# Down projection on two 64-row array tiles, paired denominators, and an earlier release of K's weights

## The chip, the cores and the metric

The kernel runs on one core of one Trainium2 chip. The metric is the device time of one execution in microseconds (us). "Before" ran at 523.56 us (median of 3 runs, 523.36 to 523.85). A ratio is the mean time of one kernel's runs over that of the other's runs in the same rounds, so it is not quite the ratio of the medians quoted beside it.

Engines are named as in the profile: PE is TensorE (PEld its weight loads), DVE VectorE, ACT ScalarE, POOL GpSimd, SP SyncE.

## The reference, cut to what matters

A linear-attention block and a GeGLU feed-forward on the same normalised input, added to the input. S = 2048 tokens, D = 576, 32 heads of 18, F = 4608, all bfloat16.

```python
xn  = layernorm(x)
q, k, v = split(xn @ wqkv);  pq, pk = phi(q), phi(k)
kv  = einsum("bhsd,bhse->bhde", pk, v);  z = sum over s of pk
att = ((pq @ kv) / (pq @ z)) @ wo
ffn = (gelu(xn @ w_gate) * (xn @ w_up)) @ w_down
out = x + att + ffn
```

## The kernel before: what the change and the argument touch

First, all tokens are normalised, K and V are reduced to the small matrix of each head and Q is made. Then there are four stages of 512 tokens, each a gate/up stage (L313, 36 feature blocks) and a down stage. The down stage multiplies the gated features `hT` with `w_down`, 36 steps, and adds five steps of attention: queries `pqT`, divided by their denominators, times `m_sb`, the product of each head's small matrix with `wo`.

The gate/up stage uses TensorE as two tiles of 64 rows. A `_Unit` has two outputs in two banks of PSUM, the memory that TensorE writes its results to. In its first phase the low rows work on output 0 and the high rows on output 1; in its second phase they change places. A relay (an empty instruction on another engine) keeps one tile from writing a bank before the other has left it.

```python
        def p1(self):                              # first phase
            for kt in self.first:
                self.mm(0, LO, kt, ...)
                last = self.mm(1, HI, kt, ...)
            self.turn = self.relay.nop()           # waits for `last`
        def p2(self):                              # second phase waits for the relay
            for kt in self.then:
                m = self.mm(1, LO, kt, ...)
                self.mm(0, HI, kt, ...)
```

The down stage uses the whole array, and so do the single denominators and the M products that are slipped in:

```python
    def down_tile(sc, j, hooks):                   # [cut]
        for hf in range(2):
            for f in range(NF):                    # 36 matmuls, 128 rows, 288 columns
                if f in todo: todo[f](acc_bank)    # an M product or a denominator
                nc.tensor.matmul(acc, lhsT=hT[:, f, ...], rhs=wd_sb[:, f, hs], ...)
            for c in range(NCH):                   # 5 more: attention
                nc.tensor.matmul(acc, lhsT=pqT[:rows, c, ts_], rhs=m_sb[:rows, c, hs], ...)
```

At the very start, the first x tiles are loaded from SP's queue and K's weights from ACT's. K's weights wait for a two-element write into their destination, which stands behind a large zero-fill on VectorE:

```python
    load_x(0, 1); load_x(1, 1); load_x(2, 2)               # SP queue: 144, 144, 288 KB
    nc.vector.memset(wqkv_sb[HP:P, 4, :], 0.0)             # 0.78 us
    nc.vector.memset(wqkv_sb[0:1, 0, D:D + 2], 0.0)        # 0.06 us
    load_w(1, nc.scalar)                                   # K's weights, 576 + 72 KB
```

## Time and profile before

| | before |
|---|---|
| median, us | 523.56 |
| TensorE's share of the chain that ended last | 97% |
| four gate/up stages | 71.33 and three times 70.04 us |
| four down stages | 42.49, 41.42, 41.42, 40.40 us |
| first gate matmul, from the span's start | 71.59 us |

The stage times are worked out from the starts of single matmuls in the trace: from the first matmul of one stage to that of the next. The views in the prediction show how TensorE's stream makes up the kernel.

### The profile page before, as it was taken

To read this page: it belongs to the slowest core of one execution; us is meant where nothing else is said; L and a number is where in the kernel's file an instruction comes from. 1 tells how busy PE (TensorE), PEld (TensorE's weight loads), DVE (VectorE), ACT (ScalarE), POOL (GpSimd) and SP (SyncE) were. 2 spreads that over 40 slices of the span, in tenths; PEclk is the share of its full clock that TensorE was granted. 3 is DMA by queue.
4 is the path that set the end of the run, shared out by engine and by line. 5 is a ranking of instruction groups with operands and counts; after the bars stand their busy time and mean duration, and the time that the engine had idled before them with its cause. 6 is when DMAs were issued, how large, how long until landed. Compare 5 with 4: busy or idle time off the path is not lost.

```text
span 521.7 us, 10641 instructions
## 1 busy us (share of the span) xinstructions
PE 516.1 (99%) x4498; PEld 313.5 (60%) x4498; DVE 250.9 (48%) x436; ACT 143.1 (27%) x293; POOL 35.2 (7%) x55
## 2 busy tenths in 40 slices
PE   7999999999999999999999999999999999999997
PEld 6777755555587754444577744444777544445775
DVE  7996565876358323433388133333584233433101
ACT  6898442332320013323200032232000123322000
POOL 2021000211001100000012000000011000000000
PEclk9999999999999999999999999999999999999999
DMA  8334609899500045555300155555100355440000
GB/s 279 62 64 118 154 25 264 254 269 266 157 12 13 13 124 155 144 156 160 93 13 13 41 166 145 155 156 155 29 23 13 103 161 158 140 134 2 13 11 24
DMA packets 106282, 57.89 MB, mean 111 GB/s; under 512 B 13370, under 2 KB 105722, under 8 KB 106234
## 3 DMA queue, kind: packets, MB, share of 16 engines
q1 hardware_dynamic: 105626, 56.55, 38.8%
q8 instruction: 35, 0.57, 0.5%
q10 hardware_dynamic: 608, 0.66, 0.4%
q14 instruction: 13, 0.11, 0.1%
HBM read 52.86 MB, written 2.36 MB: 106 GB/s over the span
## 4 chain that ended last, share of the span: by engine, by line
PE 97%; DMA 1%; ACT 1%; DVE 0%; issue 0%
PE ps_all L313 55%; PE ps_all L677 27%; PE ps_all L289 4%; PE ps_all L682 4%; PE ps_all L245 3%; PE ps_all L342 3%; DMA wqkv_sb<-in_A_wqkv_dram 1%; PE ps_all L451 1%; PE ps_all L433 0%; PE ps_all L659 0%; ACT xnT L234 0%; ACT L114 0%; ACT phi_e L265 0%; ACT phi_e L269 0%; DVE hT L273 0%; DVE res L685 0%
## 5 line engine op out<-in xcount | busy, mean ns | idle before, releaser
L313 PE MATMUL ps_all<-xnT,wg 64*128 64x512 bf16 x1152 | 272.6, 376 | 0.0
L313 PE MATMUL ps_all<-xnT,wu 64*128 64x512 bf16 x1152 | 271.8, 376 | 0.0
L648 DVE TENSOR_TENSOR hT<-ps_all,gl 128x512 bf16<-128x512 f32 x144 | 99.5, 691 | 161.9 <-ACT gl L647 161.2
L647 ACT ACTIVATE gl<-ps_all 128x512 f32<-128x512 f32 x144 | 86.1, 598 | 314.3 <-PE ps_all L313 297.4
L313 PEld LDWEIGHTS <-wu 64*128 64x128 bf16 x1152 | 108.3, 94 | 66.3
L313 PEld LDWEIGHTS <-wg 64*128 64x128 bf16 x1152 | 108.3, 94 | 66.1
L677 PE MATMUL ps_all<-wd_sb,hT 128*128 128x288 bf16 x1152 | 147.0, 286 | 0.0
L677 PEld LDWEIGHTS <-hT 128*128 128x128 bf16 x1152 | 112.3, 98 | 30.6 <-issue 1.3
L475 DVE RECIPROCAL den_sb<-den_sb 126x128 f32<-126x128 f32 (+1 forms) x80 | 68.3, 911 | 0.5
L685 DVE TENSOR_TENSOR res<-ps_all,x_sb 128x288 bf16<-128x288 f32 x32 | 14.7, 458 | 88.0 <-PE ps_all L682 88.0
L313 PE MATMUL ps_all<-xnT,wr 64*128 64x512 bf16 x288 | 55.1, 376 | 0.0
L478 POOL TENSOR_TENSOR pqT<-pqT,den_sb 126x512 bf16<-126x512 bf16 (+3 forms) x25 | 24.2, 966 | 317.3 <-DVE den_sb L475 279.4
L682 PE MATMUL ps_all<-m_sb,pqT 126*128 126x288 bf16 (+1 forms) x160 | 24.9, 285 | 0.0
L313 PEld LDWEIGHTS <-wr 64*128 64x128 bf16 x288 | 14.4, 94 | 16.9 <-issue 0.7
L245 PE MATMUL ps_all<-wqkv_sb,xnT 128*128 128x288 bf16 x160 | 22.5, 286 | 0.9 <-DMA wqkv_sb<-in_A_wqkv_dram 0.8
L289 PE MATMUL ps_all<-hT,xn 128*128 128x288 bf16 (+4 forms) x176 | 22.4, 275 | 0.0
L289 PEld LDWEIGHTS <-xn 128*128 128x128 bf16 (+1 forms) x176 | 17.5, 102 | 4.1
L245 PEld LDWEIGHTS <-xnT 128*128 128x128 bf16 x160 | 15.4, 98 | 6.9 <-issue 1.4
L682 PEld LDWEIGHTS <-pqT 126*128 126x128 bf16 (+1 forms) x160 | 15.5, 97 | 4.1
L342 PE MATMUL ps_all<-xnT,wqkv_sb 128*126 128x512 bf16 (+1 forms) x70 | 17.4, 378 | 0.0
L273 DVE SCALAR_TENSOR_TENSOR hT<-ps_all,phi_e 128x288 bf16<-128x288 f32 x32 | 13.2, 450 | 4.6 <-ACT phi_e L269 4.0
L265 ACT ACTIVATE phi_e<-ps_all 128x288 f32<-128x288 f32 x32 | 12.9, 410 | 3.6 <-PE ps_all L245 2.1
(68 smaller groups left out, 173.8 us busy)
## 6 DMA issues: line engine op xcount, KB each, us to landing
wg<-in_B_w_gate_dram SPq DMA_DIRECT2D x72, 256.0 KB, 2.9
wu<-in_B_w_up_dram SPq DMA_DIRECT2D x72, 256.0 KB, 3.5
wd_sb<-in_B_w_down_dram SPq DMA_DIRECT2D x12, 432.0 KB, 4.6
wr<-in_B_w_gate_dram SPq DMA_DIRECT2D x72, 32.0 KB, 2.7
wr<-in_B_w_up_dram SPq DMA_DIRECT2D x72, 32.0 KB, 3.1
out_dram<-res SPq DMA_DIRECT2D x15, 144.0 KB, 1.8
x_sb<-in_A_x_dram SPq DMA_DIRECT2D x3, 576.0 KB, 7.1
wqkv_sb<-in_A_wqkv_dram SPq DMA_DIRECT2D x2, 576.0 KB, 4.7
```

What stands on the lines that cost most here:

```text
L245: nc.tensor.matmul(ps_all[:, k_bank(n, hf), :HALF], lhsT=xnT[:, kt, n * P:(n + 1) * P], rhs=wqkv_sb[:, kt, D + hf * HALF:D + (hf + 1) * HALF],
L273: nc.vector.scalar_tensor_tensor(out=out_, in0=ps, scalar=0.0, in1=e, op0=ALU.max, op1=ALU.add)
L289: nc.tensor.matmul(ps_all[:m, b, col:col + w], lhsT=xn[:, n, j0:j0 + m], rhs=pk[:, n, d0:d0 + w], start=(n == 0 and col == 0), stop=(n == ...
L313: return nc.tensor.matmul(self.outs[i], lhsT=self.lhs(i, rows, kt), rhs=self.rhs(i, rows, kt), start=start, stop=stop, skip_group_check=True,)
L342: nc.tensor.matmul(ps, lhsT=wqkv_sb[:, kt, q0:q0 + rows], rhs=xnT[:, kt, sc * SC:(sc + 1) * SC], start=(kt == 0), stop=(kt == KT - 1),)
L475: nc.vector.reciprocal(out=d[:, h:h + P], in_=d[:, h:h + P])
L478: nc.gpsimd.tensor_tensor(out=pqT[:rows, c, cols], in0=pqT[:rows, c, cols], in1=d, op=ALU.mult)
L647: nc.scalar.activation(out=gl[:], in_=ps_all[:, b[0], :], func=ACT.Gelu_apprx_tanh)
L648: nc.vector.tensor_tensor(out=hT[:, GUB * k + i, :], in0=ps_all[:, b[1], :], in1=gl[:], op=ALU.mult)
L677: nc.tensor.matmul(acc, lhsT=hT[:, f, j * P:(j + 1) * P], rhs=wd_sb[:, f, hs], start=(f == 0), stop=False,)
L682: nc.tensor.matmul(acc, lhsT=pqT[:rows, c, ts_], rhs=m_sb[:rows, c, hs], start=False, stop=(c == NCH - 1),)
L685: nc.vector.tensor_tensor(out=res[:, hs], in0=acc, in1=x_sb[:, n, hs], op=ALU.add)
```

## The change

The intent: keep TensorE in its two-tile mode through the down stages too, so that it need not change mode at each end; pair the denominators; and let K's weights leave earlier by putting the large zero-fill behind them. Cut to its core:

```diff
-    nc.vector.memset(wqkv_sb[HP:P, 4, :], 0.0)
     nc.vector.memset(wqkv_sb[0:1, 0, D:D + 2], 0.0)
     load_w(1, nc.scalar)
+    nc.vector.memset(wqkv_sb[HP:P, 4, :], 0.0)
[cut]
+    nc.vector.memset(pqT[HP:P, NCH - 1, 2 * SC:], 0.0)
+    for t in (kvT, m_sb, wo2):
+        nc.vector.memset(t[HP:P, NCH - 1, :], 0.0)
[cut: den_mm, m_stage and down_tile removed]
+    def down_unit(n, b):          # one token tile: 41 steps, two halves of 288 columns
+        [cut: lhs and rhs, the slices of hT, pqT, wd_sb and m_sb for one row tile]
+        steps = range(NF + NCH)
+        return _Unit([ps_all[:, b + i, :HALF] for i in range(2)], lhs, rhs, nc.scalar, steps, steps)
+    def down_last(n, b):          # the last token tile stays on the whole array [cut]
+    def down(sc):
+        p = [banks.tiles[(banks.i + 2 * k) % 8] for k in range(4)]     # bank pairs, oldest first
+        [cut: n0, last]
+        u = [down_unit(n0 + j, p[j % 3]) for j in range(TPC - last)]
+        [cut: hooks, one table per token tile]
+        if sc == 0:
+            ms = [m_unit(c, p[3 - c % 2]) for c in range(NCH)]
+            hooks[0] = run_turns(6, ms, 9, 3, m_copy)   # from step 9, every 6; 2nd phase 3 steps later
+        [cut: one pair of denominators per token tile, first phase at step 4, second 3 steps later]
+        u[0].p1(hooks[0])
+        for j in range(1, len(u)):
+            u[j].p1(hooks[j])
+            u[j - 1].p2()
+            down_out(n0 + j - 1, u[j - 1].outs)
+        u[-1].p2()
```

More of the change, by code (lines that the diff above doesn't have):

```diff
@@ L316, in mm, with p1 @@
             )
-        def p1(self):
+        def p1(self, hooks=()):
             for kt in self.first:
+                if kt in hooks:
+                    hooks[kt]()
                 self.mm(0, LO, kt, kt == self.first[0], False)
@@ L323, in p1, with p2 @@
             tc.add_manual_dep(self.turn.ins, last.ins.name, SYNC, reason="the row tiles take turns on a bank")
-        def p2(self):
+        def p2(self, hooks=()):
             for kt in self.then:
+                if kt in hooks:
+                    hooks[kt]()
                 m = self.mm(1, LO, kt, False, kt == self.then[-1])
@@ L446, in den_evac, with part, den_pair @@
         den_sb[sc, c] = d
-    def den_mm(sc, c, bank):
-        rows = DH * HCH[c]
-        ps = ps_all[:rows, bank, :]
-        nc.tensor.matmul(ps, lhsT=zrep[:rows, c, :rows], rhs=pqT[:rows, c, sc * SC:(sc + 1) * SC], start=True, stop=True)
-        den_evac(sc, c, ps)
-    def den_pair(items, outs):
+    def part(r, c):
+        return slice(r.start, P if c == NCH - 1 else CR) if r is HI else r
+    def den_pair(items, outs, relay):
         rows = DH * HCH[items[0][1]]
-        def part(r):
-            return slice(r.start, min(r.stop, P if rows <= P - HP + 8 else rows))
         return _Unit(
             outs,
-            lambda i, r, kt: zrep[part(r), items[i][1], :rows],
-            lambda i, r, kt: pqT[part(r), items[i][1], items[i][0] * SC:(items[i][0] + 1) * SC],
-            nc.sync, first=(0,), then=(0,),
+            lambda i, r, kt: zrep[part(r, items[i][1]), items[i][1], :rows],
+            lambda i, r, kt: pqT[part(r, items[i][1]), items[i][1], items[i][0] * SC:(items[i][0] + 1) * SC],
+            relay, first=(0,), then=(0,),
         )
@@ L532 @@
     todo += [(4.0, lambda n: nc.vector.memset(x_sb[0:1, n, 0:2], 0.0), 4)]
-    todo += [(4.01, lambda n: load_x(n, 4), n) for n in (4,)]
-    todo += [(4.02, lambda n: load_w(0), 0)] + [(4.03, lambda n: load_x(n, 4), n) for n in (8, 12)]
+    todo += [(4.01, lambda n: load_x(n, 4), 4), (4.02, lambda n: load_w(0), 0)]
+    todo += [(4.03, lambda n: load_x(n, 4), n) for n in (8, 12)]
     todo.sort(key=lambda x: x[0])
@@ L641, in gu_pair @@
             items = DEN_PAIRS[k - DEN_FROM]
-            den = den_pair(items, [ps_all[:DH * HCH[c], banks.next(), :] for _, c in items])
+            den = den_pair(items, [ps_all[:DH * HCH[c], banks.next(), :] for _, c in items], nc.sync)
             den.p1()
@@ L652, in gu_pair, with m_unit, m_copy @@
                 den_evac(dsc, c, ps)
-    def m_stage(c, acc_bank):
+    def m_unit(c, b):
+        rows = DH * HCH[c]
+        return _Unit(
+            [ps_all[:rows, b + i, :HALF] for i in range(2)],
+            lambda i, r, kt: kvT[part(r, c), c, :rows],
+            lambda i, r, kt: wo2[part(r, c), c, i * HALF:(i + 1) * HALF],
+            nc.scalar, first=(0,), then=(0,),
+        )
+    def m_copy(c, u):
         rows = DH * HCH[c]
         for hf in range(2):
-            b = (acc_bank + 2 + (2 * c + hf) % 6) % 8
-            hs = slice(hf * HALF, (hf + 1) * HALF)
-            nc.tensor.matmul(
-                ps_all[:rows, b, :HALF], lhsT=kvT[:rows, c, :rows], rhs=wo2[:rows, c, hs], start=True, stop=True,
-            )
-            nc.scalar.copy(out=m_sb[:rows, c, hs], in_=ps_all[:rows, b, :HALF])
@@ L664, in down_tile, with lhs, rhs @@
-    def down_tile(sc, j, hooks):
-        n = sc * TPC + j
+            nc.scalar.copy(out=m_sb[:rows, c, hf * HALF:(hf + 1) * HALF], in_=u.outs[hf])
+    def down_unit(n, b):
+        sc, j = divmod(n, TPC)
+        ts_ = slice(n * P, (n + 1) * P)
+        def lhs(i, r, kt):
+            return hT[r, kt, j * P:(j + 1) * P] if kt < NF else pqT[part(r, kt - NF), kt - NF, ts_]
+        def rhs(i, r, kt):
+            hs = slice(i * HALF, (i + 1) * HALF)
+            return wd_sb[r, kt, hs] if kt < NF else m_sb[part(r, kt - NF), kt - NF, hs]
+        steps = range(NF + NCH)
+        return _Unit([ps_all[:, b + i, :HALF] for i in range(2)], lhs, rhs, nc.scalar, steps, steps)
@@ L666, in down_tile, with down_out @@
+    def down_out(n, outs):
+        res = fwork.tile([P, D], BF16, name="res")
+        for hf in range(2):
+            hs = slice(hf * HALF, (hf + 1) * HALF)
+            nc.vector.tensor_tensor(out=res[:, hs], in0=outs[hf], in1=x_sb[:, n, hs], op=ALU.add)
+        nc.sync.dma_start(out_view[:, n, :], res[:])
+    def down_last(n, b):
         ts_ = slice(n * P, (n + 1) * P)
         res = fwork.tile([P, D], BF16, name="res")
-        last = n == NS - 1
         for hf in range(2):
             hs = slice(hf * HALF, (hf + 1) * HALF)
-            todo = hooks.pop(0) if hooks else {}
-            acc_bank = banks.next()
-            acc = ps_all[:, acc_bank, :HALF]
+            acc = ps_all[:, b + hf, :HALF]
@@ L674, in down_tile @@
             for f in range(NF):
-                if f in todo:
-                    todo[f](acc_bank)
                 nc.tensor.matmul(
-                    acc, lhsT=hT[:, f, j * P:(j + 1) * P], rhs=wd_sb[:, f, hs], start=(f == 0), stop=False,
-                )
+                    acc, lhsT=hT[:, f, (n % TPC) * P:(n % TPC + 1) * P], rhs=wd_sb[:, f, hs], start=(f == 0), stop=False)
             for c in range(NCH):
@@ L682, in down_tile @@
                 nc.tensor.matmul(
-                    acc, lhsT=pqT[:rows, c, ts_], rhs=m_sb[:rows, c, hs], start=False, stop=(c == NCH - 1),
-                )
+                    acc, lhsT=pqT[:rows, c, ts_], rhs=m_sb[:rows, c, hs], start=False, stop=(c == NCH - 1))
             nc.vector.tensor_tensor(out=res[:, hs], in0=acc, in1=x_sb[:, n, hs], op=ALU.add)
-            if last:
-                nc.sync.dma_start(out_view[:, n, hs], res[:, hs])
-        if not last:
-            nc.sync.dma_start(out_view[:, n, :], res[:])
+            nc.sync.dma_start(out_view[:, n, hs], res[:, hs])
@@ new lines, in den_norm_all, with run_turns, end, den_out @@
+    def den_norm_all(sc, c):
+        return lambda: den_norm(sc, c, 0, 1)()
+    def run_turns(step, units, first, gap, done):
+        hooks = {}
+        for i, u in enumerate(units):
+            hooks[first + step * i] = u.p1
+            def end(u=u, i=i):
+                u.p2()
+                done(i, u)
+            hooks[first + step * i + gap] = end
+        return hooks
+    def down(sc):
+        p = [banks.tiles[(banks.i + 2 * k) % 8] for k in range(4)]
+        n0 = sc * TPC
+        last = sc == NSC - 1
+        u = [down_unit(n0 + j, p[j % 3]) for j in range(TPC - last)]
+        hooks = [{} for _ in range(TPC)]
+        if sc == 0:
+            ms = [m_unit(c, p[3 - c % 2]) for c in range(NCH)]
+            hooks[0] = run_turns(6, ms, 9, 3, m_copy)
+        if not last:
+            items = [[(sc + 1, 0), (sc + 1, 1)], [(sc + 1, 2), (sc + 1, 3)]]
+            if (sc + 1, NCH - 1) in den_sb:
+                hooks[3][4] = den_norm_all(sc + 1, NCH - 1)
+            else:
+                items.append([(sc + 1, NCH - 1), (sc + 2, NCH - 1)])
+            for k, it in enumerate(items):
+                pair = den_pair(it, [ps_all[:DH * HCH[c], p[3] + i, :] for i, (_, c) in enumerate(it)], nc.scalar)
+                def den_out(_, unit, it=it):
+                    for (dsc, c), ps in zip(it, unit.outs):
+                        den_evac(dsc, c, ps)
+                    for dsc, c in it:
+                        if dsc == sc + 1:
+                            den_norm_all(dsc, c)()
+                hooks[k + 1] = run_turns(0, [pair], 4, 3, den_out)
+        u[0].p1(hooks[0])
[4 more added lines that the diff above has]
+        u[-1].p2()
+        down_out(n0 + len(u) - 1, u[-1].outs)
+        if last:
+            down_last(NS - 1, p[0])
+        banks.i += 2
@@ L699 @@
             load_wd_slice()
-        hooks = [{6 * c_: (lambda b, c_=c_: m_stage(c_, b)) for c_ in range(NCH)} if sc == 0 else {}]
-        if sc + 1 < NSC:
-            for c_ in range(NCH):
-                def dn(b, c=c_, nsc=sc + 1):
-                    if (nsc, c) not in den_sb:
-                        den_mm(nsc, c, (b + 2) % 8)
-                    den_norm(nsc, c, 0, 1)()
-                hooks.append({0: dn})
-        for j in range(TPC):
-            down_tile(sc, j, hooks)
+        down(sc)
 _INS = ['A_x', 'A_wqkv', 'A_wo', 'B_x', 'B_w_gate', 'B_w_up', 'B_w_down']
```

## The prediction

> **What bounds the kernel now.** I read three views: the page for shares, the chain of work that ended last for stages, and the timeline for single instructions. From the page, the chain's shares and the three largest rows (line, engine, operation, output from inputs, shapes, count, then busy us, mean ns of one, idle before):
>
> ```profile
> PE 97%; DMA 1%; ACT 1%; DVE 0%; issue 0%
> L313 PE MATMUL ps_all<-xnT,wg 64*128 64x512 bf16 x1152 | 272.6, 376 | 0.0
> L677 PE MATMUL ps_all<-wd_sb,hT 128*128 128x288 bf16 x1152 | 147.0, 286 | 0.0
> L677 PEld LDWEIGHTS <-hT 128*128 128x128 bf16 x1152 | 112.3, 98 | 30.6 <-issue 1.3
> ```
>
> TensorE's matmul stream is the end of the kernel: 97% of the chain, no idle time before the large groups. The gate and up projections (L313) already run on two 64-row tiles; the down projection (L677 and L682) uses the full array. So only two things can help: fewer or closer matmul slots, or an earlier start. The chain (start us, length us, what) around one down stage and its neighbours:
>
> ```profile
> 185.48 70.04 PE ps_all L313 x648
> 255.51 4.52 PE ps_all L677 x36
> 260.03 0.62 PE ps_all L682 x5
> 260.65 0.22 PE ps_all L451
> 260.86 4.41 PE ps_all L677 x36
> ```
>
> Here 36 down matmuls take 4.41 us, 122.5 ns each, and 648 gate and up matmuls take 70.04 us, 216.2 ns a pair. The first group after the gate stage takes 4.52, not 4.41: changing to the full array costs about 0.1. The timeline shows both sides of that change and what follows it on the other engines:
>
> ```profile
> 255.14 0.38 PE L313 MATMUL ps_all<-xnT,wg 64*128 64x512 bf16 x1
> 255.45 1.15 PE L677 MATMUL ps_all<-wd_sb,hT 128*128 128x288 bf16 x8
> 255.56 0.60 ACT L647 ACTIVATE gl<-ps_all 128x512 f32<-128x512 f32 x1 [0.27 <-PE ps_all L313]
> 256.19 0.69 DVE L648 TENSOR_TENSOR hT<-ps_all,gl 128x512 bf16<-128x512 f32 x1 [0.17 <-ACT gl L647]
> ```
>
> A pair would be followed 0.216 later; the down matmul comes 0.31 later, so about 0.095 is the change. The last gate/up unit's PSUM banks stay in use until 256.19 + 0.69 = 256.88, which matters below. At the start of the kernel the timeline has:
>
> ```profile
> 0.80 1.28 ACT L114 ACT_TABLE_LOAD   x1 [0.80 <-PEq L725]
> 1.05 0.78 DVE L119 MEMSET wqkv_sb<- 64x864 uint32 x1 [1.05 <-PEq L725]
> 1.86 0.06 DVE L120 MEMSET wqkv_sb<- 1x1 uint32 x1
> 1.95 0.44 ACTq L109 DMA_DIRECT2D wqkv_sb<-in_A_wqkv_dram  x1
> 6.65 0.24 DVE L234 COPY xnT<-ps_all 128x256 bf16<-128x256 bf16 x1
> 7.41 0.77 PE L245 MATMUL ps_all<-wqkv_sb,xnT 128*128 128x288 bf16 x5 [0.79 <-DMA wqkv_sb<-in_A_wqkv_dram]
> ```
>
> K's weights are issued at 1.95, just after the one-element write ended at 1.92 and while the table load was still running to 2.08; so the write, behind a 0.78 us memset, releases them and not the table load that the chain names. They land at 7.37 and the first K matmul starts at 7.41. From 12.0 us on, the chain is nothing but TensorE up to the last matmul.
>
> **What the Trainium skill says.** (1) "TensorEngine Tiling (Array Packing)", section Key Properties: changing the tiling mode drains TensorE. The trace agrees: about 0.095 us going in, and about as much coming out (the matmul after the last L682 one starts 0.215 later where 0.1225 is usual). (2) "TensorE: Matmul & The Clock Gate", section "Wait — 56ns, not 53.3ns?": back-to-back starts are N / 2.4 GHz plus about 2.5 ns. For N = 512 that is 215.8 and for N = 288 it is 122.5; the trace's single starts have 216 for a 64-row pair and 122 to 123 for a full-array matmul. (3) The tiling page again, section "Gotcha 1: PSUM Pressure": two row tiles may not use one bank at the same time and software must order them. That is what the small relay instruction between a unit's two phases does. In the gate stage of this trace the relay starts 0.42 us after its matmul starts, 0.044 after that matmul's modelled end. (4) The clock-gate page, same section as (2): with hardware decode off, instruction handling costs about 62 ns per matmul. I use it only for a rival below.
>
> **The change, part by part.**
>
> Column count of the down projection: per token tile, before, 2 halves x 41 steps = 82 matmuls of 288 columns on 128 rows. After, each step has four 64-row matmuls, two at a time: again 82 slots of 288 columns. Contraction is a full 128 rows there, so halving it wins nothing. A pair's slot should cost what one full matmul costs: the gate pair has 512/2.4 + 2.5, with the two members 2 to 3 ns apart, so 288 gives 122.5, as now. The weight load of 94 ns starts with the previous pair, both tiles' loads together, and fits in 122.5. Gain: 0.
>
> Denominators: 14 single matmuls of 512 columns in the down stages become 7 pairs with two phases each, 14 slots of 216 ns. The rows of L451 give 0.22 for each now. Gain: under 0.1.
>
> Array changes: four entries into the down stages and three exits go away, 7 x 0.095 = 0.67. The last token tile stays on the full array, so one entry comes back: net gain 0.57, say 0.6.
>
> The M products (first down stage only): the first M unit is put into the banks of the last gate/up unit, at step 9, which is 9 x 0.1225 = 1.10 us after the stage's first matmul. Those banks come free, on the timeline above, 256.88 - 255.14 = 1.74 after the last pair starts, that is 1.52 after the next slot, plus some 0.04 for the semaphore. The built order shows the second of its matmuls waiting for VectorE there. Stall: about 0.45. Before, this cost nothing, since the banks were taken in another order. Then the last M unit finishes its second phase at step 36, and step 40 of the same unit reads its result. After that phase there are 5 slots = 0.61 us; needed are 0.29 for the matmul, 0.04, and two ScalarE copies of 0.35 each (L662: 2.8 us busy for 8), 1.1 in all. Stall: about 0.5. Before, the last M product ran at step 24 of a half, with over 1.4 us to spare. Sum of the two: +0.95.
>
> Relays: an M unit's second phase comes 3 steps after its first: 4 slots, 0.49 us. The relay needs 0.29 + 0.04 + 0.02 + some 0.04 = 0.39 and then a weight load of 0.09: just even. For a denominator pair, 0.58 against 0.38 + 0.04 + 0.02 + 0.04 + 0.09 = 0.57. I put +0.1 for all twelve together. The token tiles' own relays have a whole phase of 5 us.
>
> K's weights: the issue can come at 1.15 instead of 1.95, 0.8 earlier. Not all of that arrives: x for the first token tile is ready in transposed form only at 6.65 + 0.24 = 6.89, and in this stretch the DMA engines are about nine tenths busy from 2.1 us on, so K's packets will delay the first x tiles. I take -0.5, and it passes to the end because TensorE never waits after 12 us.
>
> The four new zero-fills: some 1,200 32-bit columns, 1.2 us on VectorE at about 54 us, where the timeline has 1.30 of idle time before the following pqT sum. Cost 0.
>
> Sum: 523.56 - 0.6 - 0.1 + 0.95 + 0.1 - 0.5 = 523.4, which I round up to 523.5.
>
> **The rivals.**
>
> (a) Four instructions for every 122.5 ns, 31 ns each, outrun TensorE's instruction handling. The gate stage shows 54 ns per instruction sustained and the present down stage 61; only short runs (25 loads and matmuls of 126 columns in 1.43 us) go at 29, and a queue may have carried these. If 62 ns per matmul were the cost, slots would be 124 ns: 1,230 x 1.5 ns = +1.8, so 525.3. If every instruction cost 35 ns, slots would be 140: +21 us, 545. Against it: the short runs show no limit, and the gate pairs keep exactly to their columns.
>
> (b) The stalls in the first down stage don't occur, or are covered, because the two row tiles slide against each other: 522.5. For it: in this trace the tiles were seen 20 ns apart at 142 us. Against it: matmuls start in program order, so a waiting one holds both tiles.
>
> (c) K's early packets only delay x, and the first K matmul waits for the transposes instead: 524.0. For it: the DMA share above. A full 0.8 instead gives 523.2.
>
> **Range and chances.** The certain terms are small: -0.6 and about +1. Startup runs from 0 to -0.8, the stalls from 0.3 to 1.2, the relays from 0 to 0.6, and (a)'s mild form adds up to 1.8. Together: 522.4 to 524.8. Over 2% means 10.5 us; no term but the strong form of (a) reaches that, 4%. Faster by 10.5 us would need denser slots than the columns allow: 1%.
>
> **What the changed profile would show.** Right: 122.5 ns between pairs of 288 columns; one gap near 0.1 instead of seven; in the first down stage a hole of about 0.45 at step 9 with VectorE's gate product as releaser and one of about 0.5 at step 40 with ScalarE's copies; the K weights' issue near 1.15 and the first K matmul near 6.9. Wrong: pairs over 125 ns apart; weight loads idle on "issue" through the down stages; waits on ScalarE's relay of over 0.1 in every unit; or the first K matmul not earlier than 7.2.

## More of the kernel before

The timeline of VectorE shows when the second x tile (tile 1) is there: its statistics start at 4.13, and no wait is noted (start us, length us, engine, line, operation):

```profile
4.13 0.46 DVE L207 BATCH_NORM_STATS2 stats<-x_sb 128x6 f32<-128x288 bf16 x1
```

The DMA view between 3 and 4 us (queue, packets started, MB, share of the 16 engines) has SP's queue as q1, with the x tiles, and ACT's as q10, with K's weights:

```profile
q1 hardware_dynamic: 127, 0.24, 94.6%
q10 hardware_dynamic: 11, 0.01, 4.5%
```

So before, the first x tiles have the DMA engines nearly to themselves until 4 us. K's weights come after them. The DMA view's row for x tile 1 (last figure: us from its issue at 1.26 to its landing):

```profile
x_sb<-in_A_x_dram SPq DMA_DIRECT2D x1, 144.0 KB, 2.3
```

## The result, and the profile after

The changed kernel took 525.78 us (median of 4, 524.65 to 526.23) against 523.68 us in the same rounds: ratio 1.0038, 95% interval 1.002 to 1.0055. It is slower by about 2 us, well inside 2%, and outside the predicted range of 522.4 to 524.8.

The page, in the rows that answer to those of before:

```profile
PE 97%; DMA 1%; ACT 1%; DVE 1%; issue 0%; SPq 0%
L313 PE MATMUL ps_all<-wd_sb,hT 64*128 64x288 bf16 x2160 | 143.7, 282 | 0.0
L313 PEld LDWEIGHTS <-hT 64*128 64x128 bf16 x2160 | 135.0, 94 | 2.2 <-issue 0.7
```

TensorE is still the chain. There are 2160 half-height matmuls in place of 1080 whole ones (15 of 16 token tiles), and they never sat idle long enough to show. Weight loads have 94 ns each and no waits to speak of.

The chain, from the first down stage to the end:

```profile
145.47 0.02 issue
145.50 0.61 ACT gl L648
146.10 0.02 issue
146.13 0.70 DVE hT L649
146.83 0.04 issue
146.87 5.48 PE ps_all L313 x82
...
152.37 358.90 PE ps_all L313 x4351
511.28 4.52 PE ps_all L700 x36
```

Twice in the first down stage the chain leaves TensorE's run: at 145.50 to 146.87 for the last gate product, and at 152.35 (in the lines left out), where ScalarE's last copy of an M product had ended at 152.32. After that 4351 matmuls follow without a break. The one change of mode that is left shows at 511.28, with 4.52 us for 36 matmuls.

Stage by stage (from the starts of single matmuls):

| | before, us | after, us | difference |
|---|---|---|---|
| start to first gate matmul | 71.59 | 74.06 | +2.47 |
| gate/up stages | 71.33, 70.04, 70.04, 70.04 | 71.23, 69.93, 69.93, 69.93 | -0.43 |
| first down stage | 42.49 | 43.19 | +0.70 |
| second and third | 41.42, 41.42 | 41.52, 41.09 | -0.23 |
| last down stage | 40.40 | 40.56 | +0.16 |

All that was meant to be the heart of the change adds up to +0.2 us, from 71.59 or 74.06 on (447.17 against 447.38 us). The loss sits before the first gate matmul. (The gate stages are shorter since the drain into the down stage was at their end; the second down stage now computes one denominator that the third computed before.)

The timeline of the start after the change:

```profile
0.86 0.06 DVE L119 MEMSET wqkv_sb<- 1x1 uint32 x1 [0.86 <-PEq L786]
0.95 0.43 ACTq L109 DMA_DIRECT2D wqkv_sb<-in_A_wqkv_dram  x1
...
6.27 0.82 DVE L207 BATCH_NORM_STATS2 stats<-x_sb 128x6 f32<-128x288 bf16 x2 [1.51 <-DMA x_sb<-in_A_x_dram]
...
7.64 0.50 PE L231 MATMUL ps_all<-ident,xn 128*128 128x128 bf16 x3 [2.67 <-DVE xn L216]
...
9.00 1.41 PE L245 MATMUL ps_all<-wqkv_sb,xnT 128*128 128x288 bf16 x5
```

K's weights are issued 1.0 us earlier, at 0.95. The statistics of x tile 1, which started at 4.13 before, now wait 1.51 us for their data and start at 6.27. They stand in front of tile 0's normalisation on VectorE, so TensorE's first transposes come at 7.64 instead of 5.49, and the first K matmul at 9.00 instead of 7.41. It no longer waits for its weights but for the tokens. The DMA view between 3 and 4 us, as shown for before:

```profile
q10 hardware_dynamic: 289, 0.33, 92.0%
q1 hardware_dynamic: 28, 0.03, 7.3%
```

The places are swapped: K's queue has the engines now, and x tile 1, issued at 1.26 as before, comes behind K. It lands 5.0 us after its issue instead of 2.3:

```profile
x_sb<-in_A_x_dram SPq DMA_DIRECT2D x1, 144.0 KB, 5.0
```

Tile 0, issued at 0.81, ahead of K, is late too, by less: its statistics start at 3.70 (3.14 before), after a wait for its data.

There is a second loss. TensorE was idle for 2.67 us before 7.64. The windows view (window, length, then busy us of PE, PEld, DVE, ACT, POOL with counts, granted clock, DMA share, GB/s) shows what that brought:

```profile
8.00:9.00 1.00, 1.00 (x12) 1.00 (x10) 0.97 (x5) 0.65 (x2) 0.21 (x1) 0.50 1.06 376
9.00:10.00 1.00, 1.00 (x7) 0.65 (x6) 1.00 (x4) 0.33 (x2) 0.24 (x1) 0.50 1.20 386
```

The granted clock (the share of TensorE's full clock, as the trace records it) is 0.50 in both, and the five K matmuls that start at 9.00 took 1.41 us where they took 0.77 before. The trace records the half clock from 7.48 to 10.89, 3.41 us.

### The profile page after: what moved, and what is told of

The parts are those of the page before. It is cut to its first block, busy times and chain, and to the rows that moved or that the text cites. A ratio compares the mean times of both kernels' runs of the same rounds, so it can differ in the third digit from the quotient of the medians.

```text
span 524.4 us, 13169 instructions
## 1 busy us (share of the span) xinstructions
PE 517.0 (99%) x5752; PEld 420.6 (80%) x5752; DVE 249.8 (48%) x440; ACT 143.3 (27%) x293; POOL 35.2 (7%) x55
## 4 chain that ended last, share of the span: by engine, by line
PE 97%; DMA 1%; ACT 1%; DVE 1%; issue 0%; SPq 0%
PE ps_all L313 84%; PE ps_all L289 4%; PE ps_all L245 3%; PE ps_all L346 3%; PE ps_all L700 2%; DMA x_sb<-in_A_x_dram 1%; PE ps_all L437 0%; ACT xnT L234 0%; PE ps_all L231 0%; PE ps_all L704 0%; PE ps_all L133 0%; DVE stats L207 0%; DVE hT L649 0%; ACT phi_e L269 0%; ACT phi_e L265 0%; ACT gl L648 0%
## 5 line engine op out<-in xcount | busy, mean ns | idle before, releaser
L313 PE MATMUL ps_all<-xnT,wg 64*128 64x512 bf16 x1152 | 275.5, 376 | 0.0
L313 PE MATMUL ps_all<-xnT,wu 64*128 64x512 bf16 x1152 | 267.5, 376 | 0.0
L313 PE MATMUL ps_all<-wd_sb,hT 64*128 64x288 bf16 x2160 | 143.7, 282 | 0.0
L313 PEld LDWEIGHTS <-hT 64*128 64x128 bf16 x2160 | 135.0, 94 | 2.2 <-issue 0.7
L313 PE MATMUL ps_all<-xnT,wr 64*128 64x512 bf16 x288 | 63.4, 376 | 0.0
L689 DVE TENSOR_TENSOR res<-ps_all,x_sb 128x288 bf16<-128x288 f32 x30 | 12.3, 452 | 64.0 <-PE ps_all L313 64.0
L313 PEld LDWEIGHTS <-wr 64*128 64x128 bf16 x288 | 22.8, 94 | 8.0
L313 PE MATMUL ps_all<-m_sb,pqT 64*128 64x288 bf16 (+1 forms) x300 | 25.9, 282 | 0.0
L449 DVE TENSOR_SCALAR den_sb<-ps_all 126x512 f32<-126x512 f32 (+1 forms) x20 | 12.8, 684 | 19.6 <-PE ps_all L313 19.6
L313 PEld LDWEIGHTS <-pqT 64*128 64x128 bf16 (+1 forms) x300 | 19.7, 94 | 0.3 <-issue 0.2
```

Source lines behind the costliest of these rows:

```text
L313: return nc.tensor.matmul(self.outs[i], lhsT=self.lhs(i, rows, kt), rhs=self.rhs(i, rows, kt), start=start, stop=stop, skip_group_check=True,)
L449: nc.vector.tensor_scalar_add(out=d[:rows, :], in0=ps, scalar1=EPS_ATT)
L689: nc.vector.tensor_tensor(out=res[:, hs], in0=outs[hf], in1=x_sb[:, n, hs], op=ALU.add)
```

## The experiments

The theory: the earlier K weights cost the whole loss, by holding up the second x tile; the two-tile down stage costs nothing by itself, and its small net loss is two waits around the M products. The rival: the two-tile down stage slows TensorE, or both share the loss. Line numbers in quoted lines shift by a few where an edit adds lines.

### 1. The down projection alone

```diff
-    nc.vector.memset(wqkv_sb[0:1, 0, D:D + 2], 0.0)
-    load_w(1, nc.scalar)
     nc.vector.memset(wqkv_sb[HP:P, 4, :], 0.0)
+    nc.vector.memset(wqkv_sb[0:1, 0, D:D + 2], 0.0)
+    load_w(1, nc.scalar)
```

> The changed kernel with the old order of the two zero-fills, so only the down projection's part is in. Theory (the early K weights cost all of the loss; the down part costs +0.2 as the two profiles' stages give, 447.38 against 447.17 us from the first gate matmul to the end): 523.9 us, ratio 1.0004, first K matmul at 7.4. Rival (the row tiles slow TensorE as a whole, or the loss is shared by both parts): 525 or more.

Measured: 523.77 us (523.37 to 524.49, 5 runs), before 523.9; ratio 0.9995 (0.9982 to 1.0008), as expected; the first K matmul came at 7.75, not 7.4, since K's weights landed later in this execution. The loss is gone. The down stages are as in the changed kernel, 43.19, 41.52, 41.09 and 40.56 us, and x tile 1 is on time again:

```profile
4.06 0.46 DVE L207 BATCH_NORM_STATS2 stats<-x_sb 128x6 f32<-128x288 bf16 x1
```

The rival falls: the two-tile down stage is worth within 1 us of nothing.

### 2. The early K weights alone

The kernel before, with only the order of the zero-fills changed (the first hunk of the change).

> The kernel before with only the order of the two zero-fills changed, so K's weights go out at about 0.95 us. Theory (K's packets get in front of the second x tile's): 525 to 525.8 us, the second tile's statistics start near 6.3 instead of 4.1, first gate matmul near 74 instead of 71.6, the down stages as before. Rival (the loss is in the down projection): 523.1, 0.5 faster than before.

Measured: 525.37 us (524.32 to 525.57, 5 runs), before 523.9; ratio 1.0022 (1.001 to 1.0034). The part alone loses 1.5 us by the medians, in the expected range, and its profile reaches the first gate matmul at 73.52 (71.59 before). The wait is the same:

```profile
5.74 0.82 DVE L207 BATCH_NORM_STATS2 stats<-x_sb 128x6 f32<-128x288 bf16 x2 [1.09 <-DMA x_sb<-in_A_x_dram]
```

The K matmuls were slow here too:

```profile
8.46 1.41 PE L245 MATMUL ps_all<-wqkv_sb,xnT 128*128 128x288 bf16 x5
```

TensorE's 38 warm-up matmuls took 4.24 us, 0.11 each (the last of them in the kernel before came 0.06 apart), and by its matmuls' spacing it did not reach full speed before about 10.5. The trace has no clock record for this stretch, so the 1.000 listed for this execution does not show it. So part of the 1.93 here is slow matmuls, as in the whole change, though the idle time before the transposes was only 1.43 us.

Tile 1 came half a us sooner here than in the profile of the whole change. The time of x tile 1 varies between executions, and so does the loss; the intervals of this ratio and of the whole change's (1.002 to 1.0055) overlap, so a remainder of some 0.5 us between the two is not settled.

### 3. Warm-up long enough to bridge the gap

```diff
-NWARM = 38
+NWARM = 72
```

> The changed kernel with 72 instead of 38 warm-up matmuls, so that TensorE has no idle 2.7 us before its first transposes. Theory (about 1.1 us of the startup loss is the half clock granted for 3.4 us after that idle time, the rest is late data): 524.7, granted clock 1.000, as the one execution of the changed kernel that had clock 1.000 (524.65). Rival (the clock plays no part): 525.8.

Measured: 525.27 us (524.98 to 525.55, 4 runs), before 523.9; ratio 1.0025 (1.0012 to 1.0038). The granted clock was 1.000 and the K matmuls took 0.80 us again, so bridging the idle time did keep the clock up. That the length of the idle time alone decides is not shown: in run 2, 1.43 us of it went with slow matmuls, as TensorE had not come up to full speed before. In the profiles, the first gate matmul comes at 72.90 here and at 74.06 unbridged; tile 1's statistics start 0.37 sooner here (5.90 against 6.27), so I estimate from these figures that the slow matmuls cost 0.8. The gain in time is 0.5 us by the medians, less than the 1.1 expected and not clear of the spread (1.002 to 1.0055 for the unbridged kernel); this expectation was a miss in size. The late data remains the larger part: with the clock repaired, the kernel is still about 1.3 us slower than before, and its first gate matmul 1.31 later.

### 4. K's weights half-way early

```diff
-    nc.vector.memset(wqkv_sb[0:1, 0, D:D + 2], 0.0)
-    load_w(1, nc.scalar)
-    nc.vector.memset(wqkv_sb[HP:P, 4, :], 0.0)
+    nc.vector.memset(wqkv_sb[HP:P, 4, 0:864], 0.0)
+    nc.vector.memset(wqkv_sb[0:1, 0, D:D + 2], 0.0)
+    load_w(1, nc.scalar)
+    nc.vector.memset(wqkv_sb[HP:P, 4, 864:], 0.0)
```

> The changed kernel with half of the large zero-fill ahead of the two-element write, so K's weights go out at about 1.4 us: after the second x tile's issue (about 1.26) and around that of the third and fourth (about 1.65). Theory (the DMA engines serve the two queues in the order of arrival, so only what is issued before K's weights is safe): the second x tile is on time, the statistics of tile 1 start near 4.1, K lands 0.3 to 0.5 earlier than before, 523.4 to 524.2. Rival (the two queues share the bandwidth whenever both are filled): about half of the loss stays, 524.8.

Measured: 524.19 us (523.63 to 525.89, 6 runs), before 523.9; ratio 1.0009 (0.9996 to 1.0022). In its profile K was issued at 1.50, after x tile 1. Tile 1's statistics started at 4.07, the first K matmul at 6.98 and the first gate matmul at 71.35, 0.24 earlier than before. Here the two queues did share: between 3 and 4 us, K's queue took 54.6% of the engines and SP's 34.5%. So plain order of arrival, as the expectation had it, is too simple; what is ahead of K on time stays on time, and what comes close behind it shares. Two of the six runs took 525 and more, so the median says little for it. The slower of the two (525.89) lists a granted clock of 0.996. The other executions with 0.996 or 0.997 are also the slowest of their kernels: three of the changed kernel (525.73 to 526.23, against 524.65 at 1.000) and one of run 2 (525.57, against 525.42 and less). That fits a stretch at half clock in each, but only that of the changed kernel's 526.23 was profiled.

### 5. A quarter of K's weights early

```diff
+    kc = slice(D, 2 * D)
     nc.vector.memset(wqkv_sb[0:1, 0, D:D + 2], 0.0)
-    load_w(1, nc.scalar)
+    nc.scalar.dma_start(wqkv_sb[:, 0, kc], A_wqkv[0:P, kc])               # 144 KB
     nc.vector.memset(wqkv_sb[HP:P, 4, :], 0.0)
+    nc.vector.memset(wqkv_sb[0:1, 1, D:D + 2], 0.0)
+    nc.scalar.dma_start(wqkv_sb[:, 1:4, kc], ...)                         # the rest
+    nc.scalar.dma_start(wqkv_sb[0:HP, 4, kc], ...)
```

> The changed kernel, but only the first quarter (144 KB) of K's weights goes out early, the other three quarters behind the large zero-fill as before the change. Theory (the second x tile waits for as many bytes as were queued before it): 144 KB take 0.4 to 0.5 us at the 300 to 390 GB/s of that stretch, so tile 1's statistics start about 0.5 later than 4.1 instead of 2.1 later, and the time is 524.0 to 524.6. Rival (any early transfer on the second queue holds the second x tile, whatever its size): 525 or more, statistics near 6.

Measured: 524.46 us (523.82 to 525.28, 5 runs), before 523.94; ratio 1.001 (0.9997 to 1.0023), in the expected range.

```profile
4.46 0.46 DVE L211 BATCH_NORM_STATS2 stats<-x_sb 128x6 f32<-128x288 bf16 x1
```

Tile 1's statistics start 0.33 later than before, against 2.14 for all of K's 648 KB, and with no wait of their own: they follow tile 0's, which start at 3.48 instead of 3.14. The data of tile 1 landed 3.0 us after its issue (2.3 before, 5.0 with all of K early). The delay grows with the bytes that are sent early. The rival, that any early transfer holds up the tile as much, whatever its size, falls.

### 6. The second x tile ahead of the early K weights

```diff
     load_x(0, 1)
-    load_x(1, 1)
+    nc.scalar.dma_start(x_sb[:, 1:2, :], x_view[:, 1:2, :])   # same queue as K, in front of it
     load_x(2, 2)
```

> The changed kernel with the second x tile issued from ScalarE's queue just ahead of K's weights, which keep their early release (issue near 1.3). Theory (arrival order decides): tile 1's statistics start by 4.1, K lands by about 6.7, first K matmul near 7.0 since the transposes of tile 0 bound it, 523.4 to 524.0. Rival (early K slows every x tile whatever the order): first gate matmul later than 72.5, 524.8 or more.

Measured: 523.64 us (523.46 to 524.07, 5 runs), before 523.94; ratio 0.9996 (0.9983 to 1.001). K's weights go out at 1.28, 0.33 later than in the changed kernel but still 0.67 earlier than before, and the loss is gone:

```profile
4.66 0.46 DVE L207 BATCH_NORM_STATS2 stats<-x_sb 128x6 f32<-128x288 bf16 x1
...
7.15 0.78 PE L245 MATMUL ps_all<-wqkv_sb,xnT 128*128 128x288 bf16 x5
```

The expectation that tile 1 would start by 4.1 was wrong: tile 0 itself came later (3.67 instead of 3.14), and tile 1's statistics follow it at 4.66. Tile 0 was late in every profile with a transfer issued on ACT's queue by 0.95, whatever it carried (3.70 in the changed kernel, 3.48 in run 5). The first K matmul is 0.26 earlier than before. Order, not an early release as such, makes the difference between 525.8 and 523.6. (The order is not all that changed: K also went 0.33 later.)

### 7. The M products moved (with the old order of the zero-fills)

```diff
-            ms = [m_unit(c, p[3 - c % 2]) for c in range(NCH)]
-            hooks[0] = run_turns(6, ms, 9, 3, m_copy)
+            ms = [m_unit(c, p[2 + c % 2]) for c in range(NCH)]
+            hooks[0] = run_turns(5, ms, 7, 3, m_copy)
```

> Down projection only (old order of the zero-fills), and the M products start in the other bank pair, at step 7, every 5 steps instead of 6, so the last is done at step 30. Theory (the first down stage lost 0.66 us to two waits: 0.37 for the gate product's bank, 0.29 for the last M product): both holes vanish, that stage takes 42.5 us instead of 43.19, and the time is 0.65 under that of the down projection alone: 523.15, ratio 0.9985. Rival (the relay or the banks put a new wait in their place): the stage stays at 43 or more.

The two waits, on TensorE's timeline of the changed kernel:

```profile
146.38 0.28 PE L313 MATMUL ps_all<-wo,kvT 64*126 64x288 bf16 x1
146.87 0.28 PE L313 MATMUL ps_all<-wo,kvT 62*126 62x288 bf16 x1 [0.20 <-DVE hT L649]
...
151.37 1.28 PE L313 MATMUL ps_all<-m_sb,pqT 64*128 64x288 bf16 x10
```

The second member of the first M unit starts 0.49 after the first, where about 0.02 is usual, released by VectorE's gate product. The ten attention matmuls last 1.28 us; with the M products moved they last 0.83:

```profile
148.98 0.83 PE L313 MATMUL ps_all<-m_sb,pqT 64*128 64x288 bf16 x10
```

Measured: 523.29 us (522.82 to 523.46, 5 runs), before 523.94; ratio 0.9986 (0.9974 to 0.9999). The first down stage takes 42.29 us instead of 43.19, so the two waits cost 0.90, more than the 0.66 I had read from the profile. By the medians the whole time is 0.48 under run 1, which was measured in other rounds; the two intervals overlap. The other stages are unchanged to 0.01 us, and the chain has no break from the Q pairs to the last token tile:

```profile
66.31 442.12 PE ps_all L313 x5166
```

From the first gate matmul to the end this is 446.47 us, 0.70 under before. That is what the two-tile down stage is worth once its waits are gone.

### 8. Both repairs

The edits of 6 and 7 together.

> Both repairs together: second x tile ahead of the early K weights, and the M products moved. If they add up: 0.65 under the run with the second x tile ahead alone, 522.8 to 523.3, ratio 0.998. If they don't, no faster than the kernel before.

Measured: 522.69 us (522.56 to 523.08, 5 runs), before 523.94; ratio 0.9979 (0.9967 to 0.9992). It is 0.95 under the run with x tile 1 ahead alone, about what the M products were found to cost in run 7 and more than the 0.65 expected, and 1.2 us under the kernel before: the fastest version here, 0.2% below the kernel before.

Single executions also showed a lone hole of 0.4 to 0.6 us at places the change doesn't touch: in runs 1 and 6 TensorE waited near 47 us for a transposing DMA, and in run 4 at 88 us for the relay on SP's queue. They are part of the spread of about 1 us within each kernel.

## Why the prediction was wrong, point by point

- **What bounds the kernel: right.** TensorE is 97% of the chain in both.
- **Slots of 288 columns: right.** Predicted gain 0. The second down stage has 328 slots of 122.5 ns and 6 of 215.8, worked out 41.47 us; it took 41.52. Rival (a), a limit on instructions, falls: four instructions per 122.5 ns were kept up through the down stages of run 7, whose chain has no break over 5166 matmuls.
- **Mode changes and denominators: right together.** Predicted -0.6 and under -0.1; with the waits removed, run 7 gained 0.70 from the first gate matmul on. The runs do not separate the two.
- **M products: right.** Predicted +0.95, in two waits of 0.45 and 0.5; removing both brought 0.90. Rival (b), that the tiles slide past these waits, falls. (The terms given for the last M unit, 0.29, 0.04 and twice 0.35, add up to 1.03, not 1.1; that moves the second wait from 0.5 to 0.4.)
- **Relays: slightly over.** Predicted +0.1. In run 7 the first stage has 338 slots of 122.5 ns and 4 of 215.8, worked out 42.27, and took 42.29; in the second and third stages some 0.05 is left over.
- **New zero-fills: right.** They took 1.2 us of VectorE from 57.11 on. In run 7, with the old start and no hole, the gate start moved by 0.53 against before and the first K matmul by 0.52.
- **K's weights: wrong, and this alone broke the prediction.** The step was "I take -0.5", with "startup runs from 0 to -0.8" for its range. The issue did come earlier, at 0.95 where 1.15 was predicted. But that K's packets delay the first x tiles was named and then priced as a discount on a gain, never as a loss: rival (c) ended at 524.0, as if the first K matmul could at worst come no earlier than before. The profile of the whole change shows +2.47 in its place, up to the first gate matmul: the first K matmul waited for the tokens and came at 9.00 (6.9 predicted; "not earlier than 7.2" was among the signs of being wrong), 1.59 later than before, and the slow matmuls make up most of the rest (the estimate in run 3). The views for it were at hand: by an estimate from the 250 to 390 GB/s of that stretch, 0.66 MB are 1.7 to 2.7 us of all DMA engines, and by the predicted 1.15, x tile 1 (issued at 1.26) would not be in its queue yet. Runs 1, 2, 5 and 6 show the mechanism: without the early release no loss, with it alone most of the loss, with 144 of the 648 KB early, tile 1's data some 0.7 late instead of 2.7, and with x tile 1 in front no loss.
- **A consequence not foreseen:** the idle TensorE fell to half clock for 3.4 us in the profiled run. Run 3 removes that and gains some 0.5 us, not clear of the spread.

Without the K part, the prediction's own sum is 523.56 - 0.6 - 0.1 + 0.95 + 0.1 = 523.9; run 1 measured 523.77.

Of the Trainium skill's places, the drain at a mode change and the spacing of N / 2.4 GHz plus 2.5 ns held in both profiles. The 62 ns per matmul of its slower decode path do not apply here: in the down stages pairs start every 122.5 ns, with no added cost that the stage sums leave room for.

## What to carry to other kernels

Before letting a transfer leave earlier, list what is issued after it and needed sooner, and price the bytes that now stand in front: here 648 KB moved ahead of a 144 KB tile that everything waited for. Splitting a full-height matmul in two half-height ones saved no slot here; it paid only by the mode changes that it avoided, so small waits at the seams (which PSUM bank comes free last, how soon a product is read) decided whether it gained. Bundled changes should be run apart: here one part hid what the other was worth.

## What the Trainium skill lacked or had wrong

- "DMA: Bandwidth & Descriptors", section "Queues, rings and completion order", says that each DMA engine goes round-robin between the queues it has work for. In the changed kernel, between 3 and 4 us, ACT's queue started 289 packets and SP's 28, though x tile 1 had been issued on SP's queue at 1.26; in run 4, with K issued 0.55 later, the shares were 54.6% and 34.5%. The page has nothing on how an earlier large transfer on one queue holds up a small later one on another (5.0 us from issue to landing here, 2.3 without). Whether that happens in the DMA engines or before them, where the list of packets is made, no run here shows.
- "TensorE: Matmul & The Clock Gate", in its closing table, gives idle gaps of over about 3 us as what throws the clock back to half. Here the gap was 2.67 us, and the trace records clock 0.50 for 3.41 us from 0.16 before its end on; with the gap bridged by 34 more warm-up matmuls it was 1.000 there.
- "TensorEngine Tiling (Array Packing)" names the drain at a mode change but no duration. Here it is about 0.095 us each way between 128 rows and two tiles of 64.
- The same page asks for software order between row tiles on one bank but gives no cost. Here a relay on ScalarE starts about 0.04 us after the modelled end of its matmul, and three steps of 122.5 ns between the phases hide it to within 0.05 us per stage.
